# A planner's costs and waits, the opening loads, and the PSUM pairs of a two-MLP kernel on one core

## Chip, core and metric

The kernel runs on one core of a Trainium2 chip. The metric is the device time of one execution in microseconds (us). TensorE is called PE here, VectorE DVE, ScalarE ACT, GpSimd POOL and SyncE SP, as in the profile. PE multiplies and writes its sums into PSUM; DVE and ACT read PSUM and work on SBUF; POOL works on SBUF only; SP issues the transfers (DMAs).

## What is computed

Retention over 4 batches, 8 heads, 768 positions and head size 64, then two MLPs with 512 inputs and 2048 hidden features on the resulting 3072 rows:

```python
for t in range(S):
    state = gamma * state + einsum('bhd,bhe->bhde', k[:, :, t], v[:, :, t])
    y[:, :, t] = scale * einsum('bhd,bhde->bhe', q[:, :, t], state)
x = y.transpose(0, 2, 1, 3).reshape(3072, 512)
h = x @ moe_w_in;  x = (h * cos(h)) @ moe_w_out
h = x @ moe2_w_in; x = where(h > 0, h, exp(min(h, 0)) - 1) @ moe2_w_out
```

The q, k and v are 32-bit floats. The four weight matrices arrive as 64-bit floats, and the kernel turns them into 32-bit ones itself.

## The kernel before

**Numbers in two parts.** Each operand of a large matmul is kept as a high and a low part, and each product is three matmuls (high x high, high x low, low x high; `PARTS`). ACT writes the high part, DVE the low one (the source minus the high part). A large matmul is 128x128 weights by 512 columns.

**Stages.** The retention works in 24 units of 128 positions of one batch (`scores`, `carried`, `values`). The first MLP's first half (`hidden`) runs over 6 blocks of 512 rows and 8 steps `j` of 256 hidden features, 24 large matmuls each, with the retention of the next block between them. Its second half (`project(0, ...)`), and both halves of the second MLP (`hidden2`, `project(1, ...)`), work on three pairs of blocks with seven products in place of eight. Each of these three stages has 1008 large matmuls.

**One step of `hidden2`.** The function `seven` writes, for three steps at once (`new`, `mid`, `old`), the products 1 (new), 4 (old), 5 (new), 7 (mid), 3 (mid), 6 (new), 2 (mid), six matmuls each. Products 1, 6, 7 and 4 of a step add up in one PSUM bank E; 5 and 3 in a bank F; 2 in a bank G that all steps share. Between products the partial sums are read: after 1, 5 and 6 an ACT pass (`snap`) copies the bank to an `h` tile; after 7, 3 and 2 DVE adds the bank to such a copy. A bank holds 128x512 numbers. The E banks of five neighbouring steps, and G, are halves of three tiles of two banks (`two`, tag `eg`): a pair holds the E of two neighbouring steps, and the third pair one E and G.

**The planner.** All work is first recorded by `Plan.op` with an engine, a duration, the tiles that it reads and writes, and a lag. `Plan.run` then plays the program through in its own time and writes out each engine's instructions in the order in which they started there. PE's order is that of the program. The others take, of what is ready, what has the earliest due time (`deadlines`); operations marked `ANY` go to DVE or POOL, whichever is free first. A transfer of 512 KB occupies SP for 1.52 us of the planner's time, and its result counts as there `LANDING` = 3.0 us later; a result of one engine can be used by another `HOP` = 0.2 us after its end. DVE and POOL running at once are both slowed by `SHARED`. Tiles come from pools with a fixed number of buffers (tag `c`: 10 of 128x1024 numbers), and a tile is written only when the planner holds its buffer for free. The framework then puts in the semaphores by its own view of which instructions touch the same tile; between two instructions on one PSUM tile of two banks it does so also where they touch different banks.

**The opening.** Transfers of the opening have ranks that set their order (`opening`): q and k of unit 0, a table `tab` of 588 columns (294 KB; its first 512 hold the decay by which q is scaled), v of unit 0, unit 1, both halves of the first weights W0 (512 KB each), units 2 and 3, W1, and then the k columns that the state sums need (here K0 to K3). PE runs scores and values of units 0 to 3 with some filler matmuls (`warm`), then `first_sums` of units 0 and 1, which read the scaled K0 and K1, and then the first half of the first `hidden` step.

## Time and profile before

| | us |
|---|---|
| median of 3 runs | 1049.24 |
| the runs | 1047.35, 1049.24, 1052.73 |
| the profiled execution | 1043.3 |
| its span, first to last instruction | 1041.5 |
| PE busy in it | 1020.3 |
| DVE busy | 762.3 |
| ACT busy | 641.6 |
| POOL busy | 195.4 |

The span is cut by PE's stages: the opening to 23.11 us, `hidden` with the retention to 340.30, `project(0)` to 568.84, `hidden2` to 806.63, `project(1)` to the end. PE's timeline shows where it stood still and what ended that; the timelines of the other engines show what they did in those moments.

### The profile page before, as it was taken

To read this page: it belongs to the slowest core of one execution; us is meant where nothing else is said; L and a number is where in the kernel's file an instruction comes from. 1 tells how busy PE (TensorE), PEld (TensorE's weight loads), DVE (VectorE), ACT (ScalarE), POOL (GpSimd) and SP (SyncE) were. 2 spreads that over 40 slices of the span, in tenths; PEclk is the share of its full clock that TensorE was granted. 3 is DMA by queue.
4 is the path that set the end of the run, shared out by engine and by line. 5 is a ranking of instruction groups with operands and counts; after the bars stand their busy time and mean duration, and the time that the engine had idled before them with its cause. 6 is when DMAs were issued, how large, how long until landed. Compare 5 with 4: busy or idle time off the path is not lost.

```text
span 1041.5 us, 17934 instructions
## 1 busy us (share of the span) xinstructions
PE 1020.3 (98%) x7077; PEld 829.8 (80%) x7080; DVE 762.3 (73%) x891; ACT 641.6 (62%) x803; POOL 195.4 (19%) x190
## 2 busy tenths in 40 slices
PE   6999999999999999999999999999999999999998
PEld 4777888888788888888887777887878888888886
DVE  5886876788689958477479888878879866556453
ACT  5983556655797643544455868988898744444441
POOL 2231540142015301000001262132123300000000
PEclk9999999999999999999999999999999999999999
DMA  9987799999999999999987569999867999998861
GB/s 338 341 325 260 259 369 325 351 334 356 335 336 361 313 340 338 358 347 311 333 293 288 220 247 324 337 340 331 295 257 267 348 317 349 331 348 312 306 217 66
DMA packets 110101, 323.39 MB, mean 310 GB/s; under 512 B 8641, under 2 KB 8641, under 8 KB 107457
## 3 DMA queue, kind: packets, MB, share of 16 engines
q1 hardware_dynamic: 110016, 322.25, 86.8%
q8 instruction: 55, 0.90, 0.3%
q14 instruction: 30, 0.24, 0.1%
HBM read 195.86 MB, written 126.35 MB: 309 GB/s over the span
## 4 chain that ended last, share of the span: by engine, by line
PE 91%; ACT 3%; DMA 2%; DVE 2%; issue 1%; SPq 0%; POOL 0%; DVEq 0%; ACTq 0%; POOLq 0%
PE eg L953 43%; PE eg L710 25%; PE eg L783 14%; PE f L783 5%; ACT c L334 2%; PE f L624 1%; PE f L657 1%; PE eg L536 1%; DMA ld<-in_attn 1%; PE eg L576 1%; DMA c<-in_weights 1%; DVE c L339 1%; DMA d<-c 1%; DVE w L441 1%; ACT h L334 1%
## 5 line engine op out<-in xcount | busy, mean ns | idle before, releaser
L953 PE MATMUL eg<-hl,w 128*128 128x512 f32 x2016 | 457.9, 389 | 1.7 <-DVE h L905 0.9
L953 PEld LDWEIGHTS eg<-hl,w 128*128 128x128 f32 x2016 | 378.3, 188 | 81.0 <-DVE h L905 1.4
L334 ACT ACTIVATE hl<-ld 128x1024 fp32r<-128x1024 f32 x168 | 178.1, 1061 | 226.6 <-PE eg L953 189.2
L339 DVE TENSOR_TENSOR hl<-ld,hl 128x1024 fp32r<-128x1024 f32 x168 | 211.5, 1268 | 93.7 <-ACT hl L334 93.5
L710 PE MATMUL eg<-hl,w 128*128 128x512 f32 x1152 | 274.1, 394 | 2.1 <-DVE c L339 1.7
L710 PEld LDWEIGHTS eg<-hl,w 128*128 128x128 f32 x1152 | 212.9, 188 | 48.1 <-issue 2.4
L339 POOL TENSOR_TENSOR c<-c 128x512 f32<-128x512 f32 (+2 forms) x116 | 133.9, 1162 | 491.4 <-DVE ld L339 160.2
L334 ACT ACTIVATE c<-c 128x512 int16<-128x512 uint32 (+3 forms) x200 | 161.0, 842 | 19.8 <-DMA c<-in_weights 12.9
L334 ACT ACTIVATE c<-eg 128x1024 int32<-128x1024 f32 (+2 forms) x95 | 86.4, 909 | 63.4 <-PE eg L710 54.6
L339 DVE TENSOR_TENSOR c<-c 128x512 f32<-128x512 f32 (+2 forms) x136 | 90.3, 674 | 47.5 <-DMA c<-d 36.2
L783 PE MATMUL eg<-hl,w 128*128 128x512 f32 x432 | 110.1, 391 | 2.6 <-ACT h L334 1.2
L783 PEld LDWEIGHTS eg<-hl,w 128*128 128x128 f32 x432 | 80.5, 188 | 21.8 <-ACT h L334 2.2
L730 DVE SCALAR_TENSOR_TENSOR c<-eg,c 128x1024 f32<-128x1024 f32 x48 | 58.6, 1221 | 30.9 <-ACT c L334 26.6
L783 PE MATMUL eg<-ld,w 128*128 128x512 f32 x288 | 73.9, 392 | 2.8 <-DVE c L339 1.7
L334 ACT ACTIVATE c<-c,quarter_turn 128x1024 f32<-128x1024 f32 x48 | 55.2, 1150 | 33.4 <-DVE c L730 32.5
L783 PEld LDWEIGHTS eg<-ld,w 128*128 128x128 f32 x288 | 53.4, 188 | 16.8 <-DVE c L339 4.0
L339 DVE TENSOR_TENSOR c<-c,eg 128x1024 f32<-128x1024 f32 x48 | 58.4, 1216 | 9.0 <-ACT c L334 8.7
L334 ACT ACTIVATE w<-c 128x1024 fp32r<-128x1024 f32 (+3 forms) x62 | 53.5, 887 | 8.9 <-DVE c L339 4.0
L441 DVE SCALAR_TENSOR_TENSOR w<-c,w 128x1024 fp32r<-128x1024 f32 (+3 forms) x51 | 57.4, 1142 | 0.2
L334 ACT ACTIVATE ends<-c 128x512 int16<-128x512 uint32 x64 | 47.1, 784 | 0.0
L334 ACT ACTIVATE h<-eg 128x512 f32<-128x512 f32 (+1 forms) x50 | 29.1, 584 | 28.5 <-PE eg L783 13.0
L339 POOL TENSOR_TENSOR ld<-ld,w 128x512 f32<-128x512 f32 x22 | 25.8, 1177 | 60.3 <-DMA ld<-in_attn 16.9
(65 smaller groups left out, 683.7 us busy)
## 6 DMA issues: line engine op xcount, KB each, us to landing
d<-c SPq DMA_DIRECT2D x205, 512.0 KB, 5.4
ld<-d SPq DMA_DIRECT2D x84, 1024.0 KB, 8.2
c<-d SPq DMA_DIRECT2D x93, 512.0 KB, 6.4
c<-in_weights SPq DMA_DIRECT2D x64, 512.0 KB, 6.5
ld<-in_attn SPq DMA_DIRECT2D x20, 1024.0 KB, 7.6
d<-h SPq DMA_DIRECT2D x48, 256.0 KB, 6.5
out<-c SPq DMA_DIRECT2D x11, 512.0 KB, 9.4
ld<-in_attn SPq DMA_DIRECT2D x3, 512.0 KB, 6.7
```

The source lines that it names most:

```text
L334: plan.op("ACT", us, lambda: nc.scalar.activation(out=out_(), in_=in_(), func=func, **kw), r, w, lag)
L339: return e.tensor_tensor(out=out_(), in0=a(), in1=b(), op=op)
L441: plan.op("DVE", 0.08 + 0.29 * (hi - lo), lambda: nc.vector.scalar_tensor_tensor(out=w.t[:, lo:hi, 1, :], in0=view(), scalar=turn, in1=hig ...
L536: nc.tensor.matmul(out=sc.t[j * D:(j + 1) * D, e, lo:lo + D], lhsT=u.t[r, 1536 + h0:1536 + h0 + D], rhs=u.t[r, 1024 + h0:1024 + h0 + D], s ...
L576: ins = nc.tensor.matmul(out=sc.t[e * HC:(e + 1) * HC, j, at:at + cols], lhsT=u.t[r, 512 + h0 + cs * HC:512 + h0 + cs * HC + HC], rhs=u.t[ ...
L624: ins = nc.tensor.matmul(out=xps[e].t[o * D:(o + 1) * D, a2, ch * HC:(ch + 1) * HC], lhsT=s[r, e * 2 + a2, :], rhs=q[r, 2 * a2 + e, ch * H ...
L657: ins = nc.tensor.matmul(out=x_out(e)[o * D:(o + 1) * D, a2, lo:lo + cols], lhsT=u.t[r, h0:h0 + D], rhs=pt.t[r, j, at:at + cols], start=(c ...
L710: nc.tensor.matmul(out=h.t[:, half * TB:(half + 1) * TB], lhsT=quarter(j, qd, wpart, kc % 2), rhs=(xh, xl)[xpart].t[:, kc, :], start=(n == ...
L730: plan.op("DVE", 1.22, lambda: nc.vector.scalar_tensor_tensor(out=g.t, in0=h.t, scalar=1.0 / TWO_PI, in1=n(), op0=ALU.mult, op1=ALU.subtra ...
L783: nc.tensor.matmul(out=out_(), lhsT=w.t[:, i, wpart, kc * P:(kc + 1) * P], rhs=x.t[:, xpart, kc, :], start=(start and n == 0), stop=(n == ...
L953: nc.tensor.matmul(out=acc.t[:, i * TB:(i + 1) * TB], lhsT=w[:, A_OF[p], wpart, i * P:(i + 1) * P], rhs=hl.t[:, gpart, k, :], start=(p in ...
```

## The change

**Planner.** `HOP` is gone. Instead an engine is busy for the spacing of its instructions (most durations get smaller, by up to a quarter: a DVE pass over 1024 columns 1.22 to 1.134, an ACT pass 1.03 to 0.965), and its result is usable `DONE` later (PE 0.21, DVE 0.14, ACT 0.16, POOL 0.11, a transfer 4.5 in place of 3.0). `SHARED` goes from 0.54 to 0.6.

**PSUM pairs.** The new `bank_of` tells the framework that a reader of one half of a `hidden2` pair and a matmul on the other half don't depend on each other.

**Opening.** The table is 172 columns (88 KB) and goes first; the 512 decay columns are one DVE product of two factors. W0 is loaded by halves, the second half of its columns ahead of unit 3 and the first half behind it, and the high and low parts of W0 are made by halves too.

The order of PE's instructions is the same, row by row. DVE gets 32 instructions more and POOL 30 fewer.

```diff
-HOP = 0.2
-SHARED = 0.54
-LANDING = 3.0
+SHARED = 0.6
+LANDING = 4.5
+DONE = {"PE": 0.21, "DVE": 0.14, "ACT": 0.16, "POOL": 0.11, "SP": LANDING}
...
-            end = min((start[m] for m in late[n]), default=now + 50.0) - HOP
-            if op[0] == "SP":
-                end -= LANDING
+            end = min((start[m] for m in late[n]), default=now + 50.0) - DONE.get(op[0], 0.14)
...
+    apart = {}
+    def bank_of(ins, r, by="read"):
+        for item in r:
+            if isinstance(item, tuple) and item[0] in apart:
+                name, half = apart[item[0]], item[1] // TB
+                tc.add_to_no_dep_group(f"{name}{half}{by}", ins.ins)
+                other = f"{name}{1 - half}{'sum' if by == 'read' else 'read'}"
+                tc.declare_no_dep(ins.ins, group=other, reason="the other bank of the pair")
+        return ins
...
-        plan.op("ACT", us, lambda: nc.scalar.activation(out=out_(), in_=in_(), func=func, **kw), r, w, lag)
+        plan.op("ACT", us, lambda: bank_of(nc.scalar.activation(out=out_(), in_=in_(), func=func, **kw), r), r, w, lag)
...
-            return e.tensor_tensor(out=out_(), in0=a(), in1=b(), op=op)
+            return bank_of(e.tensor_tensor(out=out_(), in0=a(), in1=b(), op=op), r)
...
-        for hh in range(2):
+        for hh in (1, 0) if (layer, io, j) == (0, 0, 0) else (0, 1):
+            if opening and hh == 0 and j == 0:
+                opening[0] = opening[1]
...
-                    nc.tensor.matmul(
+                    bank_of(nc.tensor.matmul(
                         out=out_(), lhsT=w.t[:, i, wpart, kc * P:(kc + 1) * P], rhs=x.t[:, xpart, kc, :],
                         start=(start and n == 0), stop=(n == 5), skip_group_check=True,
-                    )
+                    ), [r_out], "sum")
...
         two = [Buf("eg", [P, 2 * TB]) for _ in range(3)]
+        apart.update({b: f"pair{i}" for i, b in enumerate(two)})
...
+    dma(0.7, lambda: cst.t[:, 512:684], lambda: tab, w=[tab_at, cst[588, 684]])
     piece(0, 0, 1024)
-    dma(2.3, lambda: cst.t[:, 0:588], lambda: tab[:, 0:588], w=[tab_at])
+    tt("DVE", 0.65, lambda: cst.t[:, 0:512].rearrange("p (a i o) -> p a i o", a=NPAIR, i=8),
+       lambda: steps(588, 8, 8, 1), lambda: steps(620, 16, 1, 16), ALU.mult, [cst[588, 684]], [decay_at])
...
         if n == 1:
-            opening[0] = 3
+            opening[:] = [5, 7]
             first_weights(0, 30)
         elif n == 2:
-            opening[0] = 7
+            opening[0] = 9
             first_weights(1, 30)
-    opening[0] = 8
+    opening[0] = 9
```

**What moves in the order, first place: SP and DVE in the opening.** SP before (`tab`, units as `ld` and `hl`, weights as `c`; the three `ld` of 512 columns at the end are K0 to K2):

```order
L329 DMA ld<-in_attn 128x1024
L329 DMA w<-in_tab 128x588
L329 DMA ld<-in_attn 128x512
L329 DMA ld<-in_attn 128x1024
L329 DMA ld<-in_attn 128x512
L329 DMA c<-in_weights 128x1024 x2
L329 DMA ld<-in_attn 128x1024
L329 DMA ld<-in_attn 128x512
L329 DMA hl<-in_attn 128x1024
L329 DMA hl<-in_attn 128x512
L329 DMA c<-in_weights 128x1024 x2
L329 DMA ld<-in_attn 128x512 x3
```

SP now:

```order
L350 DMA w<-in_tab 128x172
L350 DMA ld<-in_attn 128x1024
L350 DMA ld<-in_attn 128x512
L350 DMA ld<-in_attn 128x1024
L350 DMA ld<-in_attn 128x512
L350 DMA ld<-in_attn 128x1024
L350 DMA ld<-in_attn 128x512
L350 DMA c<-in_weights 128x1024
L350 DMA hl<-in_attn 128x1024
L350 DMA hl<-in_attn 128x512
L350 DMA c<-in_weights 128x1024 x3
L350 DMA ld<-in_attn 128x512 x3
```

Units 2 and 3 stand ahead of one or both halves of W0 now; the K loads stand at the same place. DVE behind the mask of unit 2, before (`w<-c,w` is the low part of W0, `ld<-ld,w` the scaling of K1, `hl<-eg,hl` the low part of a unit's result):

```order
L377 SCALAR_TENSOR_TENSOR c<-c,ends 128x512
L339 TENSOR_TENSOR hl<-hl,w 128x512
L593 TENSOR_TENSOR w<-eg,w 128x768
L339 TENSOR_TENSOR w<-c,w 128x4x256
L593 TENSOR_TENSOR w<-eg,w 128x768
L339 TENSOR_TENSOR hl<-eg,hl 128x2x2x128 x2
L339 TENSOR_TENSOR ld<-ld,w 128x512
L339 TENSOR_TENSOR hl<-eg,hl 128x2x2x128
```

DVE now (`ld<-ld,w` x2 is K0 and K1):

```order
L360 TENSOR_TENSOR w<-c,w 128x2x256
L622 TENSOR_TENSOR w<-eg,w 128x768
L402 SCALAR_TENSOR_TENSOR c<-c,ends 128x512
L360 TENSOR_TENSOR hl<-eg,hl 128x2x2x128
L360 TENSOR_TENSOR w<-c,w 128x2x256
L360 TENSOR_TENSOR ld<-ld,w 128x512 x2
L360 TENSOR_TENSOR hl<-eg,hl 128x2x2x128
```

K0 has moved from POOL to DVE, behind the low part of W0's later half.

**Second place: PE in `hidden2`.** Products 1, 4, 5, 7, 3 and 6 of the fourth step (`f` is the bank F, `ld` and `hl` are the inputs), with the engine that each waits for, before:

```order
L783 MATMUL eg<-ld,w 128x512 [waits Activation_49]
L783 MATMUL eg<-ld,w 128x512 x5
L783 MATMUL eg<-hl,w 128x512 [waits DVE_49]
L783 MATMUL eg<-hl,w 128x512 x5
L783 MATMUL f<-ld,w 128x512 [waits DVE_49]
L783 MATMUL f<-ld,w 128x512 x5
L783 MATMUL eg<-hl,w 128x512 [waits Activation_49]
L783 MATMUL eg<-hl,w 128x512 x5
L783 MATMUL f<-hl,w 128x512 x6
L783 MATMUL eg<-ld,w 128x512 [waits DVE_49]
```

and now:

```order
L812 MATMUL eg<-ld,w 128x512 x6
L812 MATMUL eg<-hl,w 128x512 [waits DVE_49]
L812 MATMUL eg<-hl,w 128x512 x5
L812 MATMUL f<-ld,w 128x512 [waits DVE_49]
L812 MATMUL f<-ld,w 128x512 x5
L812 MATMUL eg<-hl,w 128x512 [waits Activation_49]
L812 MATMUL eg<-hl,w 128x512 x5
L812 MATMUL f<-hl,w 128x512 x6
L812 MATMUL eg<-ld,w 128x512 [waits Activation_49]
```

Product 1 waits for nothing now, and product 6 for ACT in place of DVE. In the built programs' semaphores, 56 of PE's waits in this stage name an instruction that reads the other half of the pair before, and none does now.

**Third place: SP in `hidden`, the second block's first steps.** The DVE pass that writes the tile c_1353 before, and c_1342 now (line 730 and 759), is the same step of the program. Its buffer was that of c_1274 before and is that of c_1038 now. SP before:

```order
L329 DMA d24_108<-c_1134 128x1024
L329 DMA ld_1276<-in_attn 128x2048
L329 DMA c_1297<-in_weights 128x1024
L329 DMA d24_108<-c_1274 128x1024
L329 DMA d0_83<-c_1153 128x1024
L329 DMA ld_1408<-in_attn 128x2048
L329 DMA d24_108<-c_1353 128x1024
```

SP now:

```order
L350 DMA d24_108<-c_1038 128x1024
L350 DMA ld_1157<-in_attn 128x2048
L350 DMA c_1199<-d24_108 128x1024
L350 DMA d24_108<-c_1140 128x1024
L350 DMA d0_83<-c_1076 128x1024
L350 DMA ld_1278<-in_attn 128x2048
L350 DMA c_1301<-d24_108 128x1024
L350 DMA d24_108<-c_1261 128x1024
L350 DMA c_1339<-in_weights 128x1024
L350 DMA d24_108<-c_1342 128x1024
```

The write-out that the pass must wait for stood three rows ahead of the write-out of its own result, and stands nine rows ahead of it now.

## Rows read from the trace of the kernel before

**Rows 1.** The page, busy time of each engine in the whole span.

```profile
PE 1020.3 (98%) x7077; PEld 829.8 (80%) x7080; DVE 762.3 (73%) x891; ACT 641.6 (62%) x803; POOL 195.4 (19%) x190
```

**Rows 2.** Busy time by stretch: length, busy (instructions), granted PE clock, DMA share, GB/s.

```profile
0.00:8.00 8.00, 5.12 (x45) 2.31 (x46) 2.38 (x8) 1.49 (x2) 0.21 (x4) 1.00 0.76 215
8.00:23.11 15.11, 9.90 (x298) 7.20 (x299) 10.21 (x14) 10.36 (x16) 4.57 (x4) 1.00 1.04 407
23.11:98.36 75.25, 73.13 (x1141) 58.32 (x1137) 60.40 (x87) 56.35 (x85) 16.61 (x24) 1.00 0.86 311
98.36:340.30 241.94, 241.94 (x2576) 195.94 (x2577) 191.95 (x253) 156.75 (x211) 74.17 (x80) 1.00 0.92 334
340.30:568.84 228.54, 228.54 (x1010) 189.25 (x1009) 161.05 (x158) 109.35 (x110) 17.54 (x11) 1.00 0.93 324
568.84:806.63 237.79, 232.39 (x1009) 187.94 (x1008) 199.58 (x249) 202.68 (x278) 72.31 (x64) 1.00 0.81 292
806.63:1041.50 234.87, 229.24 (x1009) 188.85 (x1007) 136.71 (x129) 104.66 (x104) 10.00 (x6) 1.00 0.82 288
```

**Rows 3.** PE's waits over the whole span: us in total, times, longest.

```profile
PE eg L783 <- DVE c L339: 2.3, 5, 0.7
PE eg L783 <- ACT h L334: 2.3, 3, 1.2
PE eg L710 <- DVE c L339: 1.7, 1, 1.7
PE eg L953 <- DVE h L905: 0.9, 1, 0.9
```

**Rows 4.** PE's timeline in the opening: start, us, what, idle time before it.

```profile
14.86 0.90 PE L576 MATMUL eg<-ld 64*64 64x128 f32 x32 [2.05 <-POOL ld L339]
...
21.93 1.24 PE L536 MATMUL eg<-ld 64*64 64x64 f32 x64 [0.61 <-POOL ld L339]
...
24.27 2.47 PE L710 MATMUL eg<-hl,w 128*128 128x512 f32 x10 [0.44 <-issue]
```

**Rows 5.** Timelines of ACT, DVE and POOL in the opening.

```profile
10.78 1.95 ACT L334 ACTIVATE c<-c 128x512 int16<-128x512 uint32 x3 [8.54 <-DMA c<-in_weights]
...
16.81 0.69 DVE L339 TENSOR_TENSOR hl<-hl,w 128x512 f32<-128x512 f32 x1 [0.80 <-DMA hl<-in_attn]
...
20.84 1.04 POOL L339 TENSOR_TENSOR ld<-ld,w 128x512 f32<-128x512 f32 x1 [6.02 <-DMA ld<-in_attn]
```

**Rows 6.** PE's timeline in `hidden2`, six of the places where it stood still.

```profile
572.59 3.01 PE L783 MATMUL eg<-ld,w 128*128 128x512 f32 x12 [0.87 <-ACT h L334]
...
600.48 1.65 PE L783 MATMUL eg<-ld,w 128*128 128x512 f32 x6 [0.75 <-DVE c L339]
601.98 1.52 PE L783 MATMUL eg<-hl,w 128*128 128x512 f32 x6
...
721.48 1.65 PE L783 MATMUL eg<-hl,w 128*128 128x512 f32 x6 [0.62 <-DVE h L339]
...
725.73 1.67 PE L783 MATMUL eg<-hl,w 128*128 128x512 f32 x6 [1.24 <-ACT h L334]
...
762.87 1.66 PE L783 MATMUL eg<-hl,w 128*128 128x512 f32 x6 [0.65 <-DVE c L339]
```

**Rows 7.** DVE's timeline just ahead of PE's start at 600.48.

```profile
599.75 0.68 DVE L339 TENSOR_TENSOR c<-eg,h 128x512 f32<-128x512 f32 x1
```

**Rows 8.** Timelines of SP, DVE and PE around 98 us.

```profile
87.30 0.86 SPq L329 DMA_DIRECT2D d<-c  x2
...
94.56 1.23 DVE L730 SCALAR_TENSOR_TENSOR c<-eg,c 128x1024 f32<-128x1024 f32 x1 [3.64 <-DMA d<-c]
...
98.36 1.86 PE L710 MATMUL eg<-hl,w 128*128 128x512 f32 x7 [1.69 <-DVE c L339]
```

**Rows 9.** Groups by line and shape on DVE and POOL: busy us, mean ns of one.

```profile
L339 DVE TENSOR_TENSOR c<-c 128x512 f32<-128x512 f32 x84 | 59.9, 714 | 37.8 <-DMA c<-d 32.3 <-POOL c L339 4.8
...
L339 POOL TENSOR_TENSOR c<-c 128x512 f32<-128x512 f32 x60 | 83.9, 1400 | 219.2 <-DMA c<-d 77.0 <-DVE c L885 69.9 <-DVE c L339 25.6
```

More of the change, by code (lines that the diff above doesn't have):

```diff
@@ L235, in start, with settle @@
             busy[eng] = now + us
-            heapq.heappush(events, (now + us, 0, n))
-            if eng == "SP":
-                heapq.heappush(events, (now + us + LANDING, 1, n))
+            heapq.heappush(events, (now + us, 4, n))
+            heapq.heappush(events, (now + us + DONE[eng], 1, n))
+        def settle(n, now, on_pe):
+            for m in after[n]:
+                if (ran_on[n] == "PE" and ops[m][0] == "PE") != on_pe:
+                    continue
+                need[m] -= 1
+                at[m] = max(at[m], now)
+                if need[m] == 0:
+                    able[m] = at[m]
+                    if ops[m][0] == "PE":
+                        heapq.heappush(events, (max(at[m], now), 3, 0))
+                    else:
+                        heapq.heappush(events, (max(at[m], now), 2, m))
         while events:
@@ L243, in run @@
                 _, kind, n = heapq.heappop(events)
-                if kind < 0 or (kind == 0 and ops[n][0] == "SP"):
+                if kind < 0:
+                    continue
+                if kind == 4:
+                    if ran_on[n] == "PE":
+                        settle(n, now, True)
                     continue
@@ L252, in run @@
                 if eng in ("DVE", "POOL"):
-                    if eng not in doing or doing[eng][0] != n or abs(doing[eng][4] - now) > 1e-6:
+                    if kind == 0 and (eng not in doing or doing[eng][0] != n or abs(doing[eng][4] - now) > 1e-6):
                         continue
-                    del doing[eng]
-                    pace(now)
-                    if on_port and on_port[2] == n:
-                        on_port[1] = now
+                    if kind == 0:
+                        del doing[eng]
+                        pace(now)
+                        if on_port and on_port[2] == n:
+                            on_port[1] = now
+                        heapq.heappush(events, (now + DONE[eng], 1, n))
+                        continue
                 done += 1
@@ L264, in run @@
                         heapq.heappush(events, (now, 3, 0))
-                for m in after[n]:
-                    need[m] -= 1
-                    at[m] = max(at[m], now + (0.0 if ops[m][0] == eng else HOP))
-                    if need[m] == 0:
-                        able[m] = at[m]
-                        if ops[m][0] == "PE":
-                            heapq.heappush(events, (max(at[m], now), 3, 0))
-                        else:
-                            heapq.heappush(events, (max(at[m], now), 2, m))
+                settle(n, now, False)
             for eng in ready:
@@ L391, in first_weights @@
         n = 4 * j
+        ends = [4 * j + 2] * (j == 0) + [4 * j + 4]
+        spans = []
         while n < 4 * j + 4:
-            m = min(4 * j + 4, (n // NP + 1) * NP)
+            m = min(min(x for x in ends if x > n), (n // NP + 1) * NP)
+            spans.append((n, m))
+            n = m
+        for n, m in reversed(spans) if j == 0 else spans:
             k, i, c = n // NP, n % NP, m - n
@@ L399, in first_weights @@
             low = lambda k=k, i=i, c=c: win1[k].t[:, i:i + c, 1, :]
-            act(0.1 + 0.26 * c, high, src, [t[lo, hi]], [span], lag=lag)
-            tt("DVE", 0.08 + 0.29 * c, low, src, lambda high=high: high().bitcast(F32), ALU.subtract,
+            act(0.1 + 0.215 * c, high, src, [t[lo, hi]], [span], lag=lag)
+            tt("DVE", 0.065 + 0.267 * c, low, src, lambda high=high: high().bitcast(F32), ALU.subtract,
                [t[lo, hi], span], [span], lag=lag)
-            n = m
     kept = {
@@ L595, in mask @@
                 in1=fall()[:, :, :, 0:3:2, :] if c else fall(), op=ALU.mult))
-        plan.op("DVE", 0.68 if c else 0.95, mask, [sc, fall_at], [pt], -80)
+        plan.op("DVE", 0.6 if c else 0.87, mask, [sc, fall_at], [pt], -80)
         if c == 0:
@@ L676, in values @@
             at = ((b * 2 + e) * P // 2, (b * 2 + e + 1) * P // 2) if c else (b * P, b * P + P)
-            act(0.37 if c else 0.62, lambda part=part: part(xh), src, [x], [xh[at]], lag=-80)
-            tt("DVE", 0.42 if c else 0.74, lambda part=part: part(xl), src,
+            act(0.277 if c else 0.49, lambda part=part: part(xh), src, [x], [xh[at]], lag=-80)
+            tt("DVE", 0.33 if c else 0.6, lambda part=part: part(xl), src,
                lambda part=part: part(xh).bitcast(F32), ALU.subtract, [x, xh[at]], [xl[at]], lag=-80)
@@ L862, in seven @@
             product(mid, 2, G(mid), True, g_at(mid))
-            tt("DVE", 0.7, lambda: mid.s1.t, G(mid), lambda: mid.s1.t, ALU.add,
+            tt("DVE", 0.6, lambda: mid.s1.t, G(mid), lambda: mid.s1.t, ALU.add,
                [g_at(mid), mid.s1], [mid.s1])
@@ L924, in total @@
             t = Buf("c", [P, 2 * TB])
-            tt("DVE", 1.22, lambda: t.t, lambda: buf.t, lambda: s.t, ALU.add, [buf, s], [t])
+            tt("DVE", 1.134, lambda: t.t, lambda: buf.t, lambda: s.t, ALU.add, [buf, s], [t])
             return t
@@ L1047, in retention_then_two_mlps @@
     plan.op("ACT", 1.5, lambda: nc.scalar.activation(
-        out=cst.t[:, STATE:STATE + 1], in_=rest.t[:, 0:1], func=AF.Sin), [rest], [cst[STATE, STATE + 1]])
+        out=cst.t[:, AGED:AGED + 1], in_=rest.t[:, 0:1], func=AF.Sin), [rest], [cst[AGED, AGED + 1]])
     warm(12)
```

108 lines of the change are left out of this document (56 added, 52 removed).

## The prediction

> **What bounds the kernel now.** I read the busy times first [rows 1]: PE is busy for 98% of the span, no other engine for more than 73%. So the kernel is bound by PE, and only time in which PE stands still, or is fed too slowly, can be won. The stretches say where that is [rows 2]. From 98.36 to 568.84 PE is busy all the time: nothing to win there, only to lose. The two stages of 1008 large matmuls next to each other give the cleanest measure: `project(0)` takes 228.54 us, `hidden2` takes 237.79 us for the same number of matmuls of the same shape. `hidden2` thus loses 9.25 us. The list of PE's waits names 2.3 + 2.3 us there, for DVE and ACT, and 0.6 us more (the wait of 0.62 in [rows 6]) [rows 3, 6]; the other 4 us are what a pause costs beyond its own length (after 600.48 the next product starts 1.50 us on, 601.98, where 6 x 228.54 / 1008 = 1.36 would do [rows 2, 6]) and pauses too short for the list. The rest that can be won is one wait of 1.7 us in `hidden`, 0.9 us at the very end [rows 3], and the opening up to 23.11 us, in which PE is busy for 15 us [rows 2].
>
> **Part 1, the pairs of banks.** What ends the pause at 600.48? The row says DVE c L339, and DVE's timeline has it: the add that reads bank E of step `mid` into its copy, 599.75 to 600.43 [rows 6, 7]. The waiting matmul, however, is product 6 of step `new` (it reads an `ld` tile and writes `eg`, and stands two products behind 7). It adds to the other bank of that pair, and by the planner's own dependencies owes this add nothing. The price of such a wait can be read from the code: the add needs product 7, and product 6 follows after one product (3). DVE thus has 1.36 us to do the add, at 0.68 us, between other work. With the change the add must be done by product 4 of the next step, behind 3, 6, 2 and 1: four products, 5.44 us. The copies that ACT makes have the same four products. Sorting PE's late starts in the stage by what the waiting matmul's semaphore names, ten are behind a reader of the other half (600.48 and 721.48 among them [rows 6]; each with the 0.13 us or so that its restart costs beyond it, 5.4 us in all), and three behind a reader of the matmul's own bank (572.59, 725.73 and 762.87 [rows 6], 3.7 us in all). The 5.4 us go: PE has no such wait in the new order (second place). Of the 3.7 us I take 1.6, since they are an ACT or DVE that comes late, and the new durations let the planner see such a lateness better, without removing it.
> What could come late next is DVE: in this stage it gets eight passes of 512 columns and five of 256 more, and two `h` passes of 512 fewer, by the new order. At 0.714 us for a pass of 512 [rows 9], and half of that for one of 256, this is 6 x 0.714 + 5 x 0.357 = 6.1 us on top of 199.58 of 237.79 [rows 2]. DVE has room for it (206 of about 231), but not everywhere. Bounds for the part: all of it, -9.2; or the pauses on other banks go, and half of DVE's new work turns into pauses on a bank's own readers, -5.4 + 3.1 = -2.3. I take **-7.0**, nearer to the first, because four products of room cover every DVE or ACT delay in [rows 6] but the three named.
>
> **Part 2, a longer landing.** The pause at 98.36 comes from a buffer: the DVE pass of line 730 stood for 3.64 us because its tile's buffer was still being written out by a transfer issued with the one at 87.30 [rows 8]. From there everything follows late (94.56, and PE waits 1.69 us). The planner held the transfer for landed 1.52 + 3.0 = 4.5 us after its issue; on the chip more than 6 us went by (87.30 to 94.5). With 4.5 us for the landing it reckons with 6.0. In the new order this pass gets a buffer whose write-out stands nine rows ahead on SP in place of three (third place). That pause goes: **-1.7**. The bounds are 0 (it comes back at a neighbouring step) and -1.8 with its restart. The other side of a longer landing is that buffers and loads count as taken for 1.5 us longer each; what this does is the third rival.
>
> **Part 3, the opening.** The chain there ends with K0: it lands, POOL scales it (20.84, 1.04 us), and the state sums start at 21.93 behind it [rows 4, 5]. The new order sends 294 - 88 = 206 KB less ahead of K0, at 407 GB/s [rows 2] 0.5 us, and scales K0 on DVE, whose pass of that size takes 0.69 us [rows 5]. With the 0.44 us of issue behind the sums [rows 4] the best case is -0.5 - 0.35 - 0.44 = -1.3. But K0 now stands on DVE behind the low part of W0's later half. That half has 4184 KB ahead of or in it; unit 3's q and k, 4134 KB before, landed at 16.81 [rows 5]; so about 16.9. Then come six ACT passes of 512 columns by the new order (three for W0, one for W1, the high parts of unit 2 and of W0) at 0.65 [rows 5], and two DVE passes, the low part and K0, at 0.69: 16.9 + 3.9 + 1.4 = 22.2, and the sums 0.1 later, 22.3 against 21.93. That is +0.4. I take **0**: the two sides are equally near. The decay product costs DVE one pass of 0.7 us in a stretch in which it sat waiting for the table anyway; it is hidden as long as the smaller table lands that much sooner. The filler matmuls are unchanged.
>
> **Part 4, everything else.** PE's order is unchanged, so its work is. The moved flexible passes cost nothing in the stretches where PE is always busy, as long as DVE keeps up (191.95 of 241.94 and 161.05 of 228.54 [rows 2] leave room). The 0.9 us wait at the end stays: its tile isn't among the pairs [rows 3]. Every order made anew brings some pauses that this trace can't show; I add **+1.0**, less than the largest single pause of [rows 6], 1.24, with 0 and +2.5 (two of them) as ends.
>
> **Sum.** -7.0 - 1.7 + 0 + 1.0 = -7.7 us. Against the profiled execution, 1043.3, that is 1035.6. The median of the runs is 5.9 us above that execution; carried over unchanged, 1049.2 - 7.7 = **1041.5**.
>
> **Rivals.**
> *The backlog takes the place of the wait.* Part 1 gives only -2.3: DVE and ACT are as late as before, and PE meets them one to three products later at a bank's own reader. For it: 725.73 and 762.87 are such pauses, and the stage has DVE at 84% and ACT at 85% [rows 2, 6]. Against it: the pauses at 600.48 and 721.48 were shorter than one product, so the next wait finds the work done. -2.3 - 1.7 + 1.0 = -3.0: 1046.2, no change that can be told.
> *The opening loses PE's clock.* Granted clock is 1.00 in every stretch, and the longest pause in the opening is 2.05 us [rows 2, 4]. In the new order unit 3 lands earlier and the sums don't, so PE may stand still for some 3 us ahead of 22.3. If the granted clock fell there to 1.2 GHz, the lower level, and stayed for the first 5.5 us of work, that costs half of it, 2.8 us, plus the 0.4: -7.7 + 3.2 = -4.5, 1044.7. The Trainium skill says in "TensorE: Matmul & The Clock Gate" (What's actually happening) that the array's throttled state is the default, and that only activity releases it; by that rule this rival would hold, while no run here has shown a fall.
> *Buffers held longer.* By the longer landing the planner starts passes later, and the pause of 98.36 (1.69 us) comes at many of `hidden`'s 48 steps in place of one. The DVE pass was 3.64 us late and PE lost 1.69, so some 2 us of delay are covered, and every step delayed by more pays. Slower by over 0.5% it is from the eighth step on: (7.7 + 5.25) / 1.69 = 7.7. Ten such steps in place of the one give 1041.5 + 10 x 1.69 = 1058.4. Against it: PE is busy without a break from 98.36 on, under a planner that was wrong by more.
> That the change doesn't do what it says is no rival: the waits are gone from the built program.
>
> **How the numbers follow.** Forecast 0.61 (faster), backlog 0.22 and clock 0.08 (both within 0.5%), buffers 0.09 (slower). 0.5%, 5.25 us, is about what a measurement of this kernel can tell from no change. The range runs from all bounds taken well, -9.2 - 1.8 - 1.3 = -12.3, to the backlog's time with part of the end of part 4: 1037 to 1048. It leaves out the buffers' case and the tails of the others, some 0.15.
>
> **What would show it.** `hidden2` shorter than 232 us, with no start of product 6 behind the DVE add, and the remaining pauses behind ACT's copies or DVE's adds on the bank that is written; `hidden` without the pause of 1.7 us around 98; the state sums at 21 to 22.5 us. I am wrong if `hidden2` stays above 235 us, if the granted clock is under 1.00 anywhere, or if PE waits in `hidden` or the two `project` stages by more than 3 us in all.

## The result

The changed kernel takes 1033.7 us, the median of four runs from 1033.50 to 1034.03; the kernel before, on the same chip, 1049.6 (four runs, 1047.35 to 1052.73). The ratio is 0.9866, 95% interval 0.9832 to 0.9900. The change is faster by 15.9 us, twice the forecast of 7.7, and 3.3 us beyond the low end of the range.

The profiled execution is at 1033.5, its span 1031.7. The page's busy times, to be held against [rows 1]:

```profile
PE 1018.6 (99%) x7080; PEld 832.1 (81%) x7080; DVE 776.5 (75%) x923; ACT 638.9 (62%) x804; POOL 159.9 (16%) x160
```

PE does what it did. The stretches say where the time went; they are cut by the same stages as in [rows 2] (the opening in two, `hidden` in three, `project(0)`, `hidden2`, `project(1)`; length, busy (instructions), granted clock, DMA share, GB/s):

```profile
0.00:8.00 8.00, 5.99 (x46) 2.53 (x47) 3.30 (x9) 1.49 (x2) 0.21 (x4) 1.00 0.74 223
8.00:22.49 14.49, 9.75 (x299) 7.02 (x297) 10.61 (x16) 9.83 (x17) 3.20 (x3) 0.99 1.03 403
22.49:28.03 5.54, 5.54 (x81) 4.30 (x77) 3.48 (x6) 4.74 (x8) 1.00 (x2) 0.71 1.02 387
28.03:97.00 68.97, 68.67 (x1044) 54.63 (x1041) 60.95 (x86) 52.15 (x76) 14.67 (x18) 1.00 0.84 305
97.00:339.47 242.47, 242.47 (x2612) 196.36 (x2605) 196.72 (x262) 157.65 (x213) 61.32 (x69) 1.00 0.94 338
339.47:567.95 228.48, 228.48 (x1009) 189.19 (x1008) 163.18 (x163) 109.51 (x110) 9.25 (x6) 1.00 0.92 322
567.95:797.85 229.90, 228.78 (x1010) 189.11 (x1008) 200.48 (x256) 200.20 (x280) 66.40 (x57) 1.00 0.83 303
797.85:1031.70 233.85, 228.93 (x1009) 188.92 (x1007) 137.81 (x131) 103.30 (x103) 3.88 (x3) 1.00 0.82 287
```

`hidden2` takes 229.90 us in place of 237.79 (-7.89), `project(1)` 233.85 in place of 234.87 (-1.02), the opening 22.49 in place of 23.11 (-0.62), `hidden` 316.98 in place of 317.19 (-0.21), `project(0)` -0.06. That is -9.8, profiled execution to profiled execution. The other 6.1 us of the 15.9 are not in these two traces: the median of the four runs before lies 6.3 us above the profiled execution (that of the three runs which the prediction had, 5.9 us), and now it lies 0.2 us above it.

PE's waits over the span, against [rows 3] (us in total, times, longest):

```profile
PE eg L565 <- DVE ld L360: 2.7, 1, 2.7
PE f L1054 <- DVE c L1057: 1.2, 1, 1.2
PE eg L605 <- POOL ld L360: 1.2, 1, 1.2
PE eg L812 <- ACT h L355: 1.1, 1, 1.1
PE eg L983 <- DVE h L935: 0.9, 1, 0.9
```

One wait is left in `hidden2`, behind ACT, where the first copies of the stage are made; the wait behind DVE's adds is gone, and so is the pause of [rows 8]. The wait of 0.9 at the end has stayed. New is a wait of 2.7 in the opening, with this behind it on PE's timeline (start, us, what, idle time before it):

```profile
21.26 1.30 PE L565 MATMUL eg<-ld 64*64 64x64 f32 x64 [2.69 <-DVE ld L360]
22.49 4.51 PE L739 MATMUL eg<-hl,w 128*128 128x512 f32 x12
```

Twelve large matmuls take 4.51 us there, where twelve of the same shape take 3.01 in [rows 6]. The granted clock of that stretch is 0.50, its lower level, in the window from 22.30 to 25.70 (row further down). That is the clock rival's place, at a cost of half of 3.4 us, 1.7 us. Of this 1.6 us lie in `hidden`, which without them would be 1.8 us shorter than before. All four executions show a mean granted clock of 0.998, so each lost some 2 us in this way, while the profiled execution of before had 1.000. With the clock set apart (span times mean granted clock) the two profiled executions lie 11.9 us apart, not 9.8 (1041.5 and 1029.6).

### The profile page after: what moved, and what is told of

Same layout as the page of the kernel before. It is cut to its first block, busy times and chain, and to the rows that moved or that the text cites. A ratio compares the mean times of both kernels' runs of the same rounds, so it can differ in the third digit from the quotient of the medians.

```text
span 1031.7 us, 17897 instructions
## 1 busy us (share of the span) xinstructions
PE 1018.6 (99%) x7080; PEld 832.1 (81%) x7080; DVE 776.5 (75%) x923; ACT 638.9 (62%) x804; POOL 159.9 (16%) x160
## 4 chain that ended last, share of the span: by engine, by line
PE 95%; DMA 1%; DVE 1%; ACT 1%; issue 1%; SPq 0%; DVEq 0%; ACTq 0%
PE eg L983 43%; PE eg L739 26%; PE eg L812 16%; PE f L812 6%; PE f L653 1%; PE f L686 1%; PE eg L565 1%; DMA c<-in_weights 1%; PE eg L605 1%; ACT c L355 1%; DMA ld<-in_attn 0%; DVE w L470 0%; DVE c L360 0%; ACT hl L355 0%; DVE c L402 0%
## 5 line engine op out<-in xcount | busy, mean ns | idle before, releaser
L360 DVE TENSOR_TENSOR hl<-ld,hl 128x1024 fp32r<-128x1024 f32 x168 | 208.6, 1244 | 127.2 <-ACT hl L355 126.7
L360 POOL TENSOR_TENSOR c<-c 128x256 f32<-128x256 f32 (+2 forms) x84 | 92.2, 1105 | 447.5 <-DMA c<-d 176.9
L360 DVE TENSOR_TENSOR c<-c 128x512 f32<-128x512 f32 (+2 forms) x168 | 109.8, 663 | 20.2 <-DMA c<-d 11.8
L355 ACT ACTIVATE ends<-c 128x512 int16<-128x512 uint32 x64 | 49.9, 784 | 0.5 <-DMA c<-in_weights 0.5
L360 POOL TENSOR_TENSOR h<-c 128x512 f32<-128x512 f32 x24 | 34.7, 1447 | 42.2 <-DVE c L360 19.8
```

Source lines behind the costliest of these rows:

```text
L355: plan.op("ACT", us, lambda: bank_of(nc.scalar.activation(out=out_(), in_=in_(), func=func, **kw), r), r, w, lag)
L360: return bank_of(e.tensor_tensor(out=out_(), in0=a(), in1=b(), op=op), r)
```

## The experiments

The variants ran on four chips, each group of them beside the kernel before. That took 1046.4, 1045.7, 1045.5 and 1045.8 us (74 executions, 1041.4 to 1052.0), so a few us less than beside the first result; the changed kernel took the same as there. The ratios are to the kernel before on the same chip. "Clock" is what an execution lost by its granted clock, its span times (1 - mean granted clock), averaged over the executions; "rest" is the median of the span without that, with its extremes. The clock is given to three digits, so both are good to some 0.5 us.

| kernel | us (runs) | ratio to before, 95% | clock | rest |
|---|---|---|---|---|
| before, all four chips | 1046.0 (74) | | 2.6 | 1041.9 (1037.7 to 1046.0) |
| before_again | 1046.15 (10) | 0.9992, 0.9963 to 1.0020 | 3.0 | 1040.7 (1037.3 to 1046.1) |
| only_banks | 1044.67 (10) | 0.9973, 0.9946 to 1.0000 | 4.2 | 1037.6 (1033.8 to 1040.9) |
| only_planner | 1046.34 (10) | 1.0007, 0.9987 to 1.0028 | 2.5 | 1041.8 (1041.3 to 1043.3) |
| only_opening | 1041.67 (10) | 0.9956, 0.9938 to 0.9973 | 2.2 | 1037.6 (1036.5 to 1040.6) |
| only_landing | 1046.99 (10) | 1.0004, 0.9984 to 1.0024 | 2.1 | 1043.2 (1041.1 to 1044.7) |
| without_banks | 1046.09 (10) | 0.9990, 0.9973 to 1.0008 | 2.6 | 1041.7 (1040.7 to 1042.5) |
| without_planner | 1036.46 (4) | 0.9911, 0.9887 to 0.9936 | 2.1 | 1032.4 (1030.8 to 1034.3) |
| without_opening | 1034.79 (4) | 0.9895, 0.9851 to 0.9940 | 3.1 | 1029.9 (1028.9 to 1031.7) |
| landing_back | 1036.43 (4) | 0.9907, 0.9886 to 0.9928 | 2.8 | 1031.1 (1030.6 to 1032.7) |
| after_again | 1033.78 (4) | 0.9884, 0.9848 to 0.9921 | 1.8 | 1030.1 (1029.7 to 1030.5) |
| more_fillers | 1032.27 (4) | 0.9870, 0.9835 to 0.9906 | 0.0 | 1030.5 (1030.2 to 1030.6) |
| fillers_and_tail | 1031.18 (4) | 0.9864, 0.9848 to 0.9879 | 0.0 | 1029.4 (1029.3 to 1030.0) |
| before_fillers | 1046.00 (12) | 0.9994, 0.9979 to 1.0010 | 0.2 | 1044.3 (1041.3 to 1046.1) |

### The kernel before once more: before_again

No edit.

> The kernel before, unchanged, for another profiled execution: the one that the prediction read took 1043.3 us, while the timed ones have a median of 1049.6. Theory A (the waits on the other half of a PSUM pair vary from execution to execution): about 1049 us, and hidden2 takes some 6 us more than its 237.8, the other stages the same. Theory B (buffers that the planner took for free too early, its landing of 3.0 us being too short): hidden2 about 238, and hidden or the opening some 6 us longer than 317.2 and 23.1.

Its profiled execution is at 1040.11, 3.2 us below the first one, with the same order of work, so neither theory, which each place some 6 us more, is tested by it. Its ten executions lie 10 us apart. The difference within one kernel is thus as large as the change's whole gain by the traces. The row that answers to [rows 8] is DVE's pass before PE's pause, this time 2.00 us late by the write-out of its buffer in place of 3.64:

```profile
92.51 1.23 DVE L730 SCALAR_TENSOR_TENSOR c<-eg,c 128x1024 f32<-128x1024 f32 x1 [2.00 <-DMA d<-c]
```

PE doesn't wait behind it: its next product follows on the work before it.

```profile
95.62 0.65 PE L576 MATMUL eg<-ld 64*64 64x64 f32 x32
96.32 5.72 PE L710 MATMUL eg<-hl,w 128*128 128x512 f32 x24
```

What part 2 of the prediction took for a fixed pause is one that comes out anew in each execution, and in this one not at all. (The expectation of only_landing below speaks of 0.6 us here. The only wait of PE of that length on this line in the trace, 0.62 us, is at 23.86, at the place of the 0.44 of [rows 4].) The opening varies too: it ends at 22.34 us here, at 23.11 in the first trace.

### The pairs alone: only_banks

`bank_of` and its calls put into the kernel before; every other number stays, and so does the order of the work on every engine.

```diff
+        apart.update({b: f"pair{i}" for i, b in enumerate(two)})
```

> The kernel before with the pairs of banks made independent and nothing else (the order stays as it was). Theory A: all of the gain but that of hidden and the opening, about 1036 us, and executions within 1 us of each other. Theory B: only what hidden2 lost in the profiled execution, 5 to 8 us, about 1042 us, and executions as far apart as before (5 us).

`hidden2` takes 232.95 us; the same order with dependent pairs took 237.79 and 236.70. So the waits on the other half are worth 3.8 to 4.8 us, where the prediction had put 5.4. The smaller number is nearer: the wait at the stage's start (572.59 in [rows 6]), which is on the matmul's own bank, is in the first of the three traces alone. What is left in the stage is one wait on a bank's own reader, longer than the two of before that it stands for: 2.2 us, behind ACT (PE's waits of this kernel).

```profile
PE eg L721 <- DVE c L350: 3.6, 1, 3.6
PE eg L794 <- ACT h L345: 2.2, 1, 2.2
```

The first of these rows is the pause near 98 again, in the same order of work, this time 3.6 us long; here a load came late as well (2.14 us, ahead of two passes at 92.54), and not only the write-out. DVE's row before it, PE's first product behind it, and the stretch that follows (length, busy, granted clock):

```profile
97.59 1.23 DVE L741 SCALAR_TENSOR_TENSOR c<-eg,c 128x1024 f32<-128x1024 f32 x1 [3.76 <-DMA d<-c]
```

```profile
101.40 4.93 PE L721 MATMUL eg<-hl,w 128*128 128x512 f32 x14 [3.62 <-DVE c L350]
```

```profile
101.50:105.00 3.50, 3.50 (x9) 2.75 (x10) 2.70 (x7) 0.00 (x0) 2.39 (x2) 0.56 0.09 30
```

Behind the pause the granted clock is 0.56 on average for 3.5 us, so that the pause costs some 1.5 us beyond its length. The kernel's executions lose 4.2 us to the clock on average, the most of all. Of the 4 us won in `hidden2` 1.8 show in the median (1046.4 beside it), with an interval that ends at no change. The clock, 1.6 us more than in the kernel before on average, would account for most of the difference; with losses that scatter by 2 us from execution to execution, ten runs don't prove it.

### The changed kernel with dependent pairs: without_banks

```diff
-        apart.update({b: f"pair{i}" for i, b in enumerate(two)})
```

> The changed kernel with the pairs dependent again, as before, with all else of the change. Theory A: 1033.7 + 12 = about 1046 us. Theory B: 1033.7 + 7 = about 1041 us, with hidden2 at 235 to 238 us and the other stages as in the changed kernel.

1046.09: without this one line the whole change is worth nothing that can be told. The order of the work is the one of the changed kernel on all engines, so the two traces differ by the waits alone. `hidden2` takes 241.82 us, 11.9 more than with independent pairs and 4 to 5 more than in the kernel before. PE's timeline in the stage shows the waits, ACT's copies up to 1.74 us late; in the changed kernel only the first is there:

```profile
573.23 3.01 PE L812 MATMUL eg<-ld,w 128*128 128x512 f32 x12 [1.12 <-ACT h L355]
578.36 1.66 PE L812 MATMUL eg<-hl,w 128*128 128x512 f32 x6 [0.76 <-ACT h L355]
589.91 1.65 PE L812 MATMUL eg<-hl,w 128*128 128x512 f32 x6 [1.74 <-ACT c L355]
...
646.60 1.66 PE L812 MATMUL eg<-ld,w 128*128 128x512 f32 x6 [1.29 <-ACT h L355]
...
726.18 1.66 PE L812 MATMUL eg<-ld,w 128*128 128x512 f32 x6 [1.41 <-ACT h L355]
```

The planner plans with the pairs as independent in either kernel: by its code a copy may come as late as its own bank allows, and the framework's waits then make that lateness cost. The time is that of theory A, but its `hidden2`, 4 us longer than before, is in neither theory.

### The planner alone: only_planner

The costs (the new durations, left out below), `DONE`, `LANDING` and `SHARED` of the change; the opening before, pairs dependent.

```diff
-HOP = 0.2
-SHARED = 0.54
-LANDING = 3.0
+SHARED = 0.6
+LANDING = 4.5
+DONE = {"PE": 0.21, "DVE": 0.14, "ACT": 0.16, "POOL": 0.11, "SP": LANDING}
...
```

> The kernel before with the planner's new durations, times to a usable result and landing; old opening, pairs dependent. Theory A: 1046 to 1049 us, since the waits on the other half are not in the planner's picture. Theory B: about 1041 us, executions close to each other, and no pause of 1.7 us around 98 us in hidden.

No difference in the median, as theory A had it. `hidden2` is 241.87 us with the waits of without_banks; `hidden` is at 315.68 without a pause, `project(1)` at 233.84, so the 1.0 us won in that stage is the planner's. Its gains and its loss cancel. The rests of its executions lie 2 us apart, those of the kernel before 8.

### The opening alone: only_opening

The smaller table, the halves of W0 and the load order, in the kernel before.

```diff
-    dma(2.3, lambda: cst.t[:, 0:588], lambda: tab[:, 0:588], w=[tab_at])
+    dma(0.7, lambda: cst.t[:, 512:684], lambda: tab, w=[tab_at, cst[588, 684]])
...
-        for hh in range(2):
+        for hh in (1, 0) if (layer, io, j) == (0, 0, 0) else (0, 1):
...
```

> The kernel before with the new opening alone. Theory C: within 1 us of the kernel before, about 1046 us, with executions as far apart as before. Theory D: 1043 us or less.

-4.1 us in the median, as in theory D. The opening ends at 22.52 (0.6 earlier than in the first profile, but 0.2 later than in before_again), and this trace has no pause near 98, though DVE's pass there still stands 1.35 us for a write-out (3.03 in without_planner, below). `hidden2` (237.91) and `project(1)` (234.91) are those of the kernel before. The part that I had put at 0 is the only one that is clearly worth something alone. Against the first trace of before that is the pause of 1.7 us near 98 and the 0.6 us in the opening, but before_again's trace has neither loss with the old opening. What the gain is made of, these traces don't show.

### The change without its opening, and without its planner

without_opening is the changed kernel with the old table, load order and W0 in one piece; without_planner has the old costs, `HOP`, `LANDING` and `SHARED`.

> The changed kernel with the old opening (table of 588 columns, both halves of W0 ahead of unit 2). Theory C (the pairs and the planner are worth little alone and the whole gain together, since new waits on the other half took back what the new order gave): 1033 to 1035 us, hidden2 at 230 us. Theory D (the opening is the third part without which the gain does not come): 1040 us or more.

> The kernel before with the new opening and the independent pairs, and the old planner. If the parts simply add up: the opening alone gave -4.1 us and the pairs alone -1.8 us on the timed runs, in hidden2 -4.8 us in the profile, so 1037 to 1040 us with hidden2 at 233 us. If the planner is needed for the pairs to pay (theory C): the same, some 3 us or more above the changed kernel, all of it in hidden2. If it is not needed: 1034 us.

Without the new opening 1034.79, 1.0 us above the changed kernel on the same chip, within what the two sets of four runs can tell; `hidden2` is at 229.89, as theory C had it. Without the new planner 1036.46, some 2.7 us above it (on another chip): `hidden2` is 233.38 in place of 229.90, and at the start of `project(1)` PE waits as before, a wait that the changed kernel no longer has:

```profile
803.22 37.02 PE L973 MATMUL eg<-hl,w 128*128 128x512 f32 x162 [0.72 <-DVE hl L350]
```

The planner is thus worth 3.1 to 3.5 us in `hidden2` on top of independent pairs (232.95 in only_banks and 233.38 here, to 229.90), and costs 4.1 with dependent ones (237.79 to 241.87).

This kernel has the order of work of only_opening on every engine but PE, row by row, and here the pause near 98 is back; DVE's row before it and PE's behind it:

```profile
94.50 1.23 DVE L749 SCALAR_TENSOR_TENSOR c<-eg,c 128x1024 f32<-128x1024 f32 x1 [3.03 <-DMA d<-c]
98.31 5.72 PE L729 MATMUL eg<-hl,w 128*128 128x512 f32 x24 [1.07 <-DVE c L350]
```

So the new opening doesn't remove it.

### The landing alone, there and back

In only_landing the kernel before has the new landing, in landing_back the changed kernel the old one.

```diff
-LANDING = 3.0
+LANDING = 4.5
```

> The kernel before with the landing of a transfer at 4.5 us in place of 3.0 and nothing else. Theory E (the pause near 98 us, 0.6 to 3.6 us from execution to execution, and the clock that falls behind it, come from the short landing): no such pause, executions less far apart, 1043 to 1044.5 us. Theory F (the pause is an accident of one order, which any other order loses or finds): no pause there or one elsewhere, and the time between 1041 and 1048 us, not to be told beforehand.

> The changed kernel with the landing back at 3.0 us. Theory E: a pause of 1 to 3 us for a buffer comes back in hidden, executions 3 us or more apart, 1035 to 1037 us. Theory F: within 1.5 us of the changed kernel.

only_landing gains nothing (1046.99). DVE's wait for a write-out isn't gone: it stands at the pass of line 730 one step earlier, 3.83 us long, and PE waits behind it at 92.32. `hidden2` has grown to 240.88, by more than the pause was worth. DVE's row, and PE's:

```profile
90.02 1.23 DVE L730 SCALAR_TENSOR_TENSOR c<-eg,c 128x1024 f32<-128x1024 f32 x1 [3.83 <-DMA d<-c]
92.32 5.69 PE L710 MATMUL eg<-hl,w 128*128 128x512 f32 x24 [0.80 <-DVE w L604]
```

landing_back has no pause in `hidden` at all; its time is the one that theory E gave, without the pause that was to cause it, and 2.7 us above the changed kernel where theory F allowed 1.5. So the pause near 98 isn't tied to the length of the landing. What it is tied to shows over all the traces: DVE stands for a write-out ahead of one pass of this line between 90 and 98 us in all seven traces with the old durations (1.35 to 3.83 us), whatever their landing, opening and pairs, and nowhere in `hidden` for over 1 us in the eight with the new ones, landing_back's included. Which of the new durations, `DONE` and `SHARED` does it was not taken apart. In the changed kernel the longer landing is worth some 2.5 us in the median, of which the clock accounts for 1.0 by the table; in the traces it is worth 1.4 us in `hidden2` (231.26 to 229.90) and 0.8 in `project(1)` (234.67 to 233.85).

### The changed kernel again, and with fillers in its long pause

more_fillers adds nine filler products where PE waits for K0.

```diff
         values(n - 1)
     values(3)
+    warm(9)
```

> The changed kernel, unchanged, on the chip of this call, to have it beside the parts. 1033 to 1034 us in every execution, as before. If the kernel before, measured beside it here, is near 1046.4 and not 1049.6, the ratio is nearer 0.988.

> The changed kernel with nine more filler matmuls between the values of unit 3 and the state sums, in the 2.7 us in which PE stood still there ahead of a granted clock of 0.50. If the stand-still is what made the clock fall: granted clock 1.000 and 1.5 us less, about 1032 us. If not: the clock falls all the same, and the time is that of the changed kernel.

after_again: 1033.78, as beside the first result, and 12 us below the kernel before on the same chip. The stretch behind the long pause in three traces: the changed kernel first, then after_again, then with fillers (length, busy, granted clock, DMA share, GB/s):

```profile
19.00:22.30 3.30, 1.04 (x64) 1.07 (x64) 3.04 (x6) 3.30 (x7) 0.46 (x1) 1.00 1.04 406
22.30:25.70 3.40, 3.40 (x24) 2.61 (x15) 3.37 (x7) 2.84 (x5) 1.19 (x2) 0.50 1.02 364
```

```profile
22.30:25.70 3.40, 3.40 (x47) 2.54 (x40) 3.37 (x7) 2.84 (x5) 1.24 (x2) 1.00 1.01 352
```

```profile
21.04 1.49 PE L565 MATMUL eg<-ld 64*64 64x64 f32 x64 [0.40 <-issue]
22.46 3.02 PE L739 MATMUL eg<-hl,w 128*128 128x512 f32 x12
```

In after_again's trace the pause is as long (2.85 us), and PE does 47 matmuls behind it at 1.00, not 24 at 0.50. The same kernel with the same pause loses 1.7 us in one execution and nothing in another; of its eight timed executions here and beside the first result, seven have a mean granted clock of 0.997 or 0.998. With fillers the pause is 0.40, the clock is 1.000 in all four executions, they lie within 0.4 us of each other, and the median falls by 1.5 us, to 1032.27. The fillers themselves delay nothing: the first product of `hidden` starts at 22.46, against 22.48 and 22.49.

### Both kernels beaten: fillers_and_tail

more_fillers, and the two halves of the last PSUM tile of `project(1)` independent too. That tile's wait of 0.9 us [rows 3] is of the kind of part 1: the matmuls of one half wait for the copy of the other.

```diff
+                plan.op("DVE", 0.33, lambda src=src, lo=lo, hi=hi, at=at: bank_of(nc.vector.tensor_copy(
...
+            if halves:
+                apart[acc] = "tail"
...
+                                    if len(ii) == 1:
+                                        bank_of(ins, [acc[i * TB, i * TB + TB]], "sum")
```

> The changed kernel with the nine fillers, and with the two halves of the last PSUM tile independent too, so that PE need not wait 0.93 us for the copy of the first half near the end. Granted clock 1.000, no wait of PE for the copy: 1032.3 - 0.9 = about 1031.3 us.

1031.18 us, 1.1 below more_fillers; `project(1)` takes 232.59 in place of 233.83, and the wait behind line 935 is gone from the list:

```profile
PE eg L605 <- POOL ld L360: 1.8, 1, 1.8
PE f L1058 <- DVE c L1061: 1.2, 1, 1.2
PE eg L812 <- ACT h L355: 1.1, 1, 1.1
PE eg L565 <- issue: 0.8, 2, 0.6
```

### Fillers in the kernel before: before_fillers

What was open after these runs was the distance of 5.9 us between the profiled execution of before and its median.

```diff
-            for _ in range(n):
+            for _ in range(n if n > 3 else 9):
```

> The kernel before with nine filler products where it had three in each group of fillers of the opening; the planner still counts three, so the order of the work is the same on every other engine. Theory S (the spread of the kernel before, and the distance of its median from its quickest executions, come mostly from falls of the granted clock behind pauses of TensorE in the opening): the mean granted clock is 0.999 or 1.000 in nearly all executions, they lie within 3 us of each other, and the median is 2 to 3 us below the kernel before of the same call (1043 where that is 1045.7). Theory B (they come from the wait for a buffer near 98 us, which these fillers don't touch): the granted clock of the executions stays scattered between 0.99 and 1.00, and the median stays within 1 us of the kernel before. If the granted clock is full and executions are still scattered over 5 us or more, then what scatters them is time at full clock.

Half of each theory came in. The granted clock is 0.999 or 1.000 in all 12 executions, where the kernel before loses 2.6 us on average: nearly all that its clock loses are thus falls behind pauses of the opening. But the median is the same, since the rest grew by 2.2 us beside the kernel before on the same chip. The fillers stand in PE's way in this order. The scores of unit 3, at 19.18 and 20.42 in the kernel before, come behind them at 20.77 and 21.48, and the first product of `hidden` starts at 24.52 in place of 23.11:

```profile
18.95 1.89 PE L1024 MATMUL f<-c 128*128 128x512 bf16 x8 [0.16 <-issue]
20.77 0.90 PE L657 MATMUL eg<-w,ld 64*64 64x128 f32 x32
21.48 0.85 PE L657 MATMUL eg<-w,hl 64*64 64x128 f32 x32
...
23.70 0.89 PE L536 MATMUL eg<-ld 64*64 64x64 f32 x32 [0.90 <-DVE ld L339]
```

And with the clock full the executions still lie 4 us apart (1043.81 to 1047.83), as the 11 of the kernel before at 1.000 do (1043.36 to 1046.73). This trace has the pause near 98 at 3.27 us, with a load 2.91 us late ahead of it and the granted clock at 1.00 behind it, and one of 1.78 us in `project(1)` that the two traces of the kernel before don't have (only_banks, of the same order, has 0.96 us there):

```profile
100.83 4.36 PE L710 MATMUL eg<-hl,w 128*128 128x512 f32 x18 [3.27 <-DVE c L339]
```

```profile
960.95 74.87 PE L953 MATMUL eg<-hl,w 128*128 128x512 f32 x329 [1.78 <-DVE hl L339]
```

Behind the second one, too, stands a transfer. ACT's high part of the tile had waited 5.79 us for its load (3.15 is its longest wait for a load in this stage of the first profile of before, and only_banks has 4.94 there). DVE stood 3.39 us for a write-out ahead of the low part that PE needs, but in the first profile of before it did so for 3.36 us, with no wait of PE behind it (third row):

```profile
952.23 2.01 ACT L334 ACTIVATE hl<-ld 128x1024 fp32r<-128x1024 f32 x2 [5.79 <-DMA ld<-d]
```

```profile
957.93 0.69 DVE L339 TENSOR_TENSOR h<-c 128x512 f32<-128x512 f32 x1 [3.39 <-DMA d<-h]
```

```profile
953.26 0.69 DVE L339 TENSOR_TENSOR h<-c 128x512 f32<-128x512 f32 x1 [3.36 <-DMA d<-h]
```

The scatter beside the clock is thus, where a trace shows it, waits for transfers that land later in one execution than in another, at places where the order leaves no room. Why a transfer lands later in one execution, no run shows.

## Why the prediction was wrong

**The step that failed** is one sentence of the sum: "The median of the runs is 5.9 us above that execution; carried over unchanged". I treated the 5.9 us as something that every kernel has; in the changed kernel the distance is 0.2 us. On the four chips the kernel before has a median of 1046.0, 2.7 us above the execution that I read, and the clock accounts for about that much: its executions lose 2.6 us on average to falls of the granted clock, and the one that I read had 1.000. The changed kernel loses about as much (1.8 us in after_again, some 2 in all four executions of the result), but its profiled execution shows that loss already, so nothing of it is left to add. The other 3.2 us are those by which the kernel before took longer beside the first result than later; only 24 of the 74 later executions reach even the lowest of those four. Why is open: falls and late transfers of that size were found, but no trace of such an execution was taken, and no granted clock of those four runs is on record.

The sum itself, against the profiled execution, gave 1035.6, and that execution is at 1033.5. This nearness is in part luck: the parts brought 3.8 us more than I had summed, and the clock, which the sum has no term for, took 1.7 back.

Beside the clock the kernel before scatters, by 8 us (the column "rest"), the changed kernel by 0.8 in after_again. The kernels with the old durations lie 3.5 to 9 us apart there (7 with the pairs alone, 4 with the opening or the landing alone), those with the new ones 0.4 to 2.8, the same division as in the wait for the write-out near 98. That this wait is all of the scatter is not shown; the one in `project(1)` is another.

**Part 1, -7.0: -7.89 measured.** The mechanism held: the waits on the other half are gone, and without_banks brings them back. The split was off. The waits on other halves were worth 3.8 to 4.8 alone, not 5.4, and the planner gave 3.1 to 3.5 on top where I had taken 1.6 of the waits on a bank's own reader. The rows could have told: PE was idle for 5.4 us in the whole stage (237.79 less 232.39 [rows 2]), 2.8 of them in the three waits on its own banks [rows 6], so at most 2.6 on other halves, and ten restarts of 0.13 us make that 3.9. More important is what the split hid: the parts don't add. The planner costs 4.1 us without the pairs and gains 3.1 to 3.5 with them, so the pairs are worth 4 us in the old order and 11.9 in the new one. I had priced them in the old order only. DVE's extra work of 6.1 us in `hidden2` didn't come: 200.48 us busy against 199.58, with 7 passes more in place of 11 (256 and 249 [rows 2]). DVE's extra passes lie ahead of it: it is busy for 275.1 us up to the end of `hidden`, in place of 264.9 (the first five rows of the stretches above, and the first four of [rows 2]).

**Part 2, -1.7: right in size against the trace that I read, wrong in cause.** The pause is gone, and one of 0.30 us at 38.14 has come; that `hidden` is only 0.21 us shorter is the clock's 1.6 us. But the longer landing alone only moves DVE's wait for a write-out one step ahead, the bound that I had put at 0, and with the landing taken back it doesn't return: by all the traces it goes with the planner's other new costs. I also read a pause of one execution as a fixed price; the same order gave none, 1.7, 3.3 and 3.6 us.

**Part 3, 0: -0.6, and -4.1 alone in the median.** The state sums start at 21.26, not at 22.3, so the passes in front of K0 cost 1 us less than I had summed. The 0.6 us is within what executions differ by: the opening ends at 22.34 to 24.75 us in the six traces with the old one and its own fillers, at 22.06 to 23.39 in the eight with the new one. For the rest of the 4.1 us I had no term, and what it is stays open.

**Part 4, +1.0: 0.3 of new pauses, and -1.0 in `project(1)`.** New pauses are all but absent. And the wait of 0.72 us at the start of `project(1)`, with its restart, went with the planner; I had read only the larger one at the end of that stage [rows 3].

**The rivals.** The backlog did not come: one wait of 1.12 us in `hidden2` is left. Buffers held longer did not come. The clock did come, at the place and after a pause of the length named (2.69 us against "some 3 us"), at 1.7 us in place of 2.8, and in seven of eight executions. "I am wrong if the granted clock is under 1.00 anywhere" was therefore too strict: it fell, and the kernel won all the same. The Trainium skill, "TensorE: Matmul & The Clock Gate" (What's actually happening), takes the lower clock for the state that only activity lifts; the 0.50 behind the pause and the 1.000 with fillers agree with it, and after_again's 1.00 behind a pause of 2.85 us shows that such a pause need not end in a fall.

## What to carry to other kernels

A single trace is one draw: before a forecast is moved from a trace to a median, ask what the distance between the two is made of (granted clock of each run, waits on transfers), and whether the change removes it. Price a false wait in the order that the change will have, not in the one that is there; a planner that doesn't know of the framework's waits made them dearer here (by 4 us) as its other estimates got better. Where PE had to wait for data anyway, fillers were free and held the clock at 1.000; where they stood ahead of work that was due, they cost what they gave.

## What the chip showed beside

- The same pause of PE in the same program, 2.69 and 2.85 us long, was followed by a granted clock of 0.50 in one execution and of 1.00 in another. So was the pause near 98 in one order of work: 0.56 behind 3.62 us, 1.00 behind 3.27 us.
- One DVE pass waited 3.64, 2.00, 3.76 and 2.23 us for the write-out of its buffer in four executions with the same order of work on every engine but PE, and PE waited 1.69, 0, 3.62 and 3.27 us behind it; in the last two a load ahead of the pass was late as well.
